# Five more items of the head each carry a step of a weight conversion, in a kernel of attention and two MLPs

## The chip, the cores and the metric

One core of a Trainium2 chip runs the whole program. The metric is the device time of one execution in microseconds; lower is better. The engines are PE (matrix products), DVE, ACT and POOL (elementwise work) and SP (which only issues transfers). Each engine has its own instruction stream and works it off in order. Sixteen DMA engines move the data.

## The reference

Causal attention with a decaying bias, then a leaky MLP, then four experts that are weighed by probabilities:

```python
scores = scale * np.matmul(q, k.transpose(0, 1, 3, 2))          # 2 batches, 8 heads, 576 positions, 64 wide
cum = np.cumsum(np.maximum(s, 0.0), axis=-1)
scores = np.where(causal, -1e9, scores + np.minimum(-(cum[..., :, None] - cum[..., None, :]), 0.0))
attn = softmax(scores)
x = matmul(attn, v)                                              # laid out as 1152 tokens x 512
h = x @ w_in                                                     # 512 x 2048
x = np.maximum(0.01 * h, h) @ w_out                              # 2048 x 512
for e in range(4):
    out += p[:, e:e + 1] * (np.maximum(x @ w1[e], 0.0) @ w2[e])
```

`w_in` and `w_out` come as 64-bit floats. The kernel gets their bits as pairs of 32-bit words and makes 32-bit floats of them on the chip: this is the conversion that the change is about.

## The kernel before, in words

**Attention as items.** Attention is cut into 16 units: a pair of heads of one batch, units 0 to 7 for positions up to 256, units 8 to 15 for the rest. A unit of the first kind has four items, one of the second kind five (its first item is the short last tile of both heads). `attention()` (line 1005) runs over the items `i` and issues, by the table `STEPS` (line 1003), different steps of different items together: the scores of item i on PE, followed by a mask and a row minimum on DVE (tile `z`), the exponentials of item i-1 on ACT (`z` in place), the transposes of item i-3 on PE (`ps_pt`) with their copies on ACT (`pv`), the products with the values of item i-5 (`ps_o`), and what ends a unit after that (`xo`, `ps_x`, `x`). It yields three times per item; between the yields its caller puts other work.

**The head.** The caller's first loop (line 1069 and on) runs over items 0 to 39 and is called the head here. Up to item 17 it puts idle products on PE, from item 24 on, by the table `OPENED`, the first steps of the MLP (`ps_u<-x,w`, three products of 512 columns each), from item 31 on two idle products more per item. At the third yield of an item it calls the conversion's generator once, if the item's number stands in the table `CONVERTING`, and at every item from 31 on.

**The woven stage.** The second loop runs over the items that are left, to 79. It puts about one step of the MLP's first half at two of the three yields, and calls the conversion at two yields of most items. When attention is over, the MLP goes on alone; its second half works on sums and differences of x (tile `t`) that DVE makes in `paired_steps`.

**The conversion.** `supply()` (line 151) converts 16 pieces of 128 x 1024 numbers, one step per call: the absolute value on ACT (`raw<-r`), two steps that clamp and shift on DVE (TENSOR_SCALAR on `raw`), two that join the low and the sign bits on DVE (SCALAR_TENSOR_TENSOR `raw<-r,raw`). The input `r` of a piece is fetched by `fetch64` (line 122) with two buffers: the fetch of piece n+2 is issued right behind the writing of piece n to memory (`w_f<-raw`, in `send`), on ACT's queue while `heading` is true, on POOL's queue after it. In the head the sending and splitting of piece n stand between the first and the second step of piece n+1, so that a piece takes seven calls there and six in the woven stage.

**The split.** A product needs a weight as a rounded part and a rest: a cast on ACT (`w<-raw`) and a subtraction on DVE (`w<-raw,w`). A piece that is next in line while one of the four weight buffers (`WB`) is free is split by `supply` straight from `raw`. Otherwise `late_splits()` (line 128) reads it back from memory on SP's queue (`raw<-w_f`) and splits it in two halves.

**The order.** All of this part is issued in the order in which the program is written (`InOrder`, line 28), so the tables decide what stands behind what on each engine. A profile names every such instruction by the one line 43.

Of the kernel before, what the change touches and what calls it, by code (L numbers as in the profile page):

```python
# [19 lines left out]
def attention_moe_moe2(ctx: ExitStack, tc: tile.TileContext, q, k, v, s, w_in, w_out, probs, w1, w2, out):  # L20
# [107 lines left out]
    def late_splits():  # L128

        nonlocal reading  # L130
        while len(ready) < CONVERTED:
            n = len(ready)
            if n < min(retired + WB + 2, stored):
                reading, raw = True, kept.pop(n, None)
                if raw is None:
                    raw = load_w(*stream[n][:3])
                    for _ in range(5):
                        yield
                while n >= retired + WB:
                    yield  # L140

                w = wpool.tile([P, 2, 1024], F32R, tag="w", name="w")
                for part in (slice(0, 512), slice(512, 1024)):
                    nc.scalar.copy(w[:, 0, part], raw[:, part])
                    (nc.gpsimd if n == CONVERTED - 1 else nc.vector).tensor_tensor(w[:, 1, part], raw[:, part], f32(w[:, 0, part]), ALU.subtract)
                ready.append(w.rearrange("p l (a b) -> p l a b", a=stream[n][1][0]))
                reading = False
            else:
                yield
# [900 lines left out]
    with ExitStack() as phase:  # L1050
# [3 lines left out]

        OPENED = (24, 25, 26, 27, 28, 29, 31, 33, 35)

        CONVERTING = (*range(5, 16), *range(17, 31, 2))
        side, units_of_w, late, opened = attention(), supply(), late_splits(), 0
        nothing = ps_mm.tile([P, 512], F32, tag="mm", name="nothing")
        with tc.tile_pool(name="early", bufs=1) as early:  # L1060
# [5 lines left out]
            for at_ in range(3 * 64):  # L1066
# [13 lines left out]
                if at_ % 3 == 2:  # L1080
                    if i == 3:
                        fetch64(1)
                    if i in (3, 4, 5):
                        next(sums)
                    if i in CONVERTING or i >= 31:
                        next(units_of_w)
# [109 lines left out]
```

## Time and profile before

| | |
|---|---|
| median of 3 runs | 698.78 us (698.61 to 701.58) |
| the profiled execution | 699.07 us, of which the span from the first to the last instruction is 697.3 us |
| PE busy | 677.7 us, 97% of the span |
| DVE, ACT, POOL busy | 475.8, 352.5, 406.0 us |
| mean granted clock of PE | 0.998 |

Times in the trace are counted from the start of the span. Busy time of PE is made of matmuls whose ends are modelled, so a busy PE may still hold short waits; a gap that the trace shows is real idle time. A row of a timeline gives start, length, engine, instruction, how many are merged in it, and in brackets the idle time before it and what ended that. A wait for several events is put down to the one that came last.

### The profile page before, as it was taken

The numbers are of one execution on the slowest core, as the hardware profiler recorded it, in microseconds if no ns is written. First come the engines' busy times: TensorE is split into PE (matmuls) and PEld (weight loads), VectorE is DVE, ScalarE is ACT, GpSimd is POOL, SyncE is SP. The second block draws the span as 40 slices with busy tenths as digits, with TensorE's granted clock in tenths as the row PEclk, the third lists the DMA queues.
The fourth block names the chain that finished last, engine by engine and source line by source line (L and its number), as shares of the span: only waits on it lengthen the run. The fifth ranks groups of instructions, "written<-read, shape, count | busy, mean of one in ns | idle before, by whom it ended". The sixth has DMA issues, their size and how long they took to land.

```text
span 697.3 us, 12008 instructions
## 1 busy us (share of the span) xinstructions
PE 677.7 (97%) x4496; PEld 623.7 (89%) x4496; DVE 475.8 (68%) x1040; ACT 352.5 (51%) x727; POOL 406.0 (58%) x386
## 2 busy tenths in 40 slices
PE   8899999899998999999999999999999999999998
PEld 7778778778787999999999989999899899998997
DVE  6878899998697458837855747647657376465564
ACT  5768978876544566533634525325244253261520
POOL 5100212221198887861997949949679498495830
PEclk9999999999999999999999999999999999999999
DMA  7798689746631321101011110111202111112003
GB/s 217 197 244 205 198 224 276 218 154 211 241 122 62 121 91 62 62 1 61 1 61 62 61 61 30 63 31 61 61 1 62 61 34 58 32 62 61 1 16 120
DMA packets 43050, 69.15 MB, mean 99 GB/s; under 512 B 6432, under 2 KB 26672, under 8 KB 42992
## 3 DMA queue, kind: packets, MB, share of 16 engines
q1 hardware_dynamic: 33744, 40.30, 19.9%
q0 software_dynamic: 6016, 20.71, 9.6%
q10 hardware_dynamic: 3232, 7.38, 3.3%
q8 instruction: 35, 0.57, 0.4%
q14 instruction: 23, 0.19, 0.1%
HBM read 57.54 MB, written 10.82 MB: 98 GB/s over the span
## 4 chain that ended last, share of the span: by engine, by line
PE 71%; DVE 8%; issue 8%; DMA 7%; ACT 3%; POOL 2%; SPq 0%; ACTq 0%; POOLq 0%; DVEq 0%
PE ps_d L43 35%; PE ps_u L43 33%; DMA r<-in_moe_w_out_dram 3%; DVE t L43 2%; DMA qr<-in_q_dram 2%; DMA r<-in_moe_w_in_dram 1%; PE ps_sc L43 1%; DVE sums L43 1%; DVE raw L43 1%; PE ps_o L43 1%; DVE z L43 1%; PE ps_pt L43 1%; DMA ke<-cum 1%; ACT raw L43 1%; DVE y L43 1%
## 5 line engine op out<-in xcount | busy, mean ns | idle before, releaser
L43 PE MATMUL ps_u<-t,w 128*128 128x320 f32 (+1 forms) x1680 | 237.7, 301 | 4.1 <-DVE t L43 2.9
L43 POOL TENSOR_TENSOR w<-raw,w 128x512 fp32r<-128x512 f32 (+2 forms) x118 | 185.9, 1595 | 94.2 <-ACT w L43 93.9
L43 PEld LDWEIGHTS ps_u<-t,w 128*128 128x128 f32 x1680 | 231.4, 191 | 5.5 <-DVE t L43 3.2
L43 PE MATMUL ps_d<-w,ht 128*128 128x256 f32 (+1 forms) x1164 | 195.4, 326 | 0.1
L43 PEld LDWEIGHTS ps_d<-w,ht 128*128 128x128 f32 x1164 | 173.3, 190 | 18.6 <-PE ps_u L43 0.4
L43 ACT CAST w<-raw 128x512 fp32r<-128x512 f32 (+2 forms) x138 | 98.2, 740 | 127.0 <-PE ps_d L43 69.7
L43 ACT ACTIVATE ht<-ps_u 128x320 fp32r<-128x320 f32 (+2 forms) x160 | 68.6, 439 | 99.2 <-DVE ps_u L43 71.1
L43 PE MATMUL ps_d<-ht,w 128*128 128x320 f32 (+1 forms) x576 | 109.1, 340 | 0.2 <-DVE ht L43 0.2
L43 PEld LDWEIGHTS ps_d<-ht,w 128*128 128x128 f32 x576 | 91.4, 188 | 6.6 <-DVE ht L43 0.6
L43 POOL TENSOR_TENSOR raw<-raw 128x256 f32<-128x256 f32 x120 | 86.2, 741 | 1.9
L43 DVE SCALAR_TENSOR_TENSOR oacc<-ps_d,pn,oacc 128x256 f32<-128x256 f32 (+1 forms) x92 | 51.5, 578 | 44.9 <-PE ps_d L43 44.2
L43 DVE TENSOR_TENSOR ps_u<-ps_u,tmp 128x320 f32<-128x320 f32 (+1 forms) x120 | 55.8, 469 | 31.5 <-PE ps_u L43 29.9
L43 DVE SCALAR_TENSOR_TENSOR ht<-ps_u,ht 128x320 fp32r<-128x320 f32 (+1 forms) x112 | 49.8, 455 | 16.8 <-ACT ht L43 16.5
L43 DVE TENSOR_TENSOR tmp<-ps_u,tmp 128x320 f32<-128x320 f32 (+1 forms) x80 | 36.9, 462 | 32.0 <-PE ps_u L43 24.5
L43 POOL DMA_DIRECT2D w_f<-raw x13 | 8.3, 637 | 85.3 <-DVE raw L43 71.8
L43 PE MATMUL ps_u<-x,w 128*128 128x512 f32 x192 | 55.7, 410 | 0.9 <-DVE x L43 0.9
L43 ACT ACTIVATE z<-z,mn 128x256 f32<-128x256 f32 (+4 forms) x72 | 42.5, 590 | 8.7 <-DVE mn L43 7.8
L43 DVE TENSOR_TENSOR ht<-ps_u,ht 128x320 fp32r<-128x320 f32 (+1 forms) x48 | 26.5, 553 | 26.8 <-ACT ps_u L43 26.6
L43 DVE CUSTOM_DVE_ANT_0 z<-ps_sc,mask 128x256 f32<-128x256 f32 (+4 forms) x72 | 35.9, 499 | 10.1 <-PE ps_sc L43 6.6
L43 POOL TENSOR_TENSOR ht<-sums,ht 128x1024 fp32r<-128x1024 f32 x16 | 38.6, 2409 | 6.3 <-ACT ht L43 6.3
L43 ACT COPY pv<-ps_pt 128x512 f32<-128x512 f32 (+3 forms) x80 | 33.2, 424 | 15.8 <-PE ps_pt L43 15.7
L43 PE MATMUL ps_pt<-ident,z 128*128 128x128 f32 x200 | 34.6, 276 | 5.9 <-ACT pv L43 4.9
(97 smaller groups left out, 773.5 us busy)
## 6 DMA issues: line engine op xcount, KB each, us to landing
raw<-in_moe_w_dram SPq DMA_DIRECT2D x32, 512.0 KB
raw<-w_f SPq DMA_DIRECT2D x21, 512.0 KB
w_f<-raw POOLq DMA_DIRECT2D x13, 512.0 KB, 3.5
r<-in_moe_w_out_dram POOLq DMA_DIRECT2D x6, 1024.0 KB, 8.6
r<-in_moe_w_in_dram POOLq DMA_DIRECT2D x5, 1024.0 KB, 8.4
r<-in_moe_w_in_dram ACTq DMA_DIRECT2D x3, 1024.0 KB
kd<-in_k_dram POOLq DMA_DIRECT2D x8, 288.0 KB, 7.6
kr<-in_k_dram SPq DMA_DIRECT2D x8, 288.0 KB
```

Source lines behind the costliest of these rows:

```text
L43: ins = call(*args, **kw)
```

## The change

Items 18, 20, 22, 24 and 26 of the head carry a call of the conversion too. Nothing else is edited.

```diff
-        CONVERTING = (*range(5, 16), *range(17, 31, 2))
+        CONVERTING = (*range(5, 16), *range(17, 28), 29)
```

The head then makes 31 calls in place of 26, and each later call comes five calls earlier against the items. Piece 2 (counted from 0) begins at item 18 instead of 19 and ends at item 24 instead of 31; piece 3 begins at item 25 instead of 32; the first three steps of piece 4 lie in the head. The order of PE's instructions is the same before and after. On SP the transfers `raw<-w_f` grow from 21 to 26, since pieces 4, 5, 8, 9 and 10 go through `late_splits` now; on ACT's queue `w_f<-raw` grows from 3 to 4 and `r<-in_moe_w` from 5 to 6, on POOL's queue they shrink by one each.

**First place: ACT at items 18 to 20.** `x0` is an output of attention, `raw_502` (`raw_487` in the change) is piece 2, `raw_347` piece 1, `r64` the 64-bit input. Before:

```order
L43 CAST x0_108<-ps_x_483 128x256
L43 ACTIVATE z_472<-z_472,mn_473 128x128
L43 COPY pv0_102<-ps_pt_497 128x256
L43 ACTIVATE raw_502<-r64_363 128x1024
L43 ACTIVATE z_487<-z_487,mn_488 128x128
L43 COPY pv0_102<-ps_pt_520 128x256
L43 ACTIVATE z_514<-z_514,mn_515 128x256
L43 COPY pv1_103<-ps_pt_536 128x128
L43 DMA w_f32_76<-raw_347 128x1024
L43 DMA r64_543<-in_moe_w_out_dram 128x2x1024
L43 CAST w_545<-raw_347 128x1024
```

In the change:

```order
L43 CAST x0_108<-ps_x_483 128x256
L43 ACTIVATE raw_487<-r64_363 128x1024
L43 ACTIVATE z_472<-z_472,mn_473 128x128
L43 COPY pv0_102<-ps_pt_499 128x256
L43 DMA w_f32_76<-raw_347 128x1024
L43 DMA r64_505<-in_moe_w_out_dram 128x2x1024
L43 CAST w_507<-raw_347 128x1024
L43 ACTIVATE z_489<-z_489,mn_490 128x128
L43 COPY pv0_102<-ps_pt_525 128x256
L43 ACTIVATE z_519<-z_519,mn_520 128x256
L43 COPY pv1_103<-ps_pt_542 128x128
```

The absolute value of piece 2 stands ahead of one exponential and one copy more, and the cast of piece 1 stands two exponentials and two copies earlier.

**Second place: DVE at items 21 to 24.** Before:

```order
L43 TENSOR_TENSOR xo_528<-ps_o_467,st_525 128x256
L43 ISA z_530,mn_531<-ps_sc_532,mask_93 128x256
L43 ISA mn_531 128x1
L43 ISA z_548,mn_549<-ps_sc_550,mask_93 128x128
L43 ISA mn_549 128x1
L43 ISA z_563,mn_564<-ps_sc_565,mask_93 128x128
L43 ISA mn_564 128x1
L43 TENSOR_TENSOR x0_108<-ps_x_559,x0_108 128x256
L43 TENSOR_TENSOR w_545<-raw_347,w_545 128x1024
```

In the change:

```order
L43 TENSOR_TENSOR xo_533<-ps_o_467,st_530 128x256
L43 TENSOR_TENSOR w_507<-raw_347,w_507 128x1024
L43 ISA z_536,mn_537<-ps_sc_538,mask_93 128x256
L43 ISA mn_537 128x1
L43 TENSOR_SCALAR raw_487<-raw_487 128x1024
L43 ISA z_550,mn_551<-ps_sc_552,mask_93 128x128
L43 ISA mn_551 128x1
L43 TENSOR_SCALAR raw_487<-raw_487 128x1024
L43 ISA z_566,mn_567<-ps_sc_568,mask_93 128x128
L43 ISA mn_567 128x1
L43 TENSOR_TENSOR x0_108<-ps_x_561,x0_108 128x256
L43 SCALAR_TENSOR_TENSOR raw_487<-r64_363,raw_487 128x1024
```

The subtraction of piece 1 stands ahead of item 21's `z` instead of behind item 23's, and steps of piece 2 stand between the `z` rows that followed each other before.

**Third place: ACT in the woven stage, unit 14.** `pv0` of 128x4x2x64 is the first copy out of the five transposes of a unit's first item. Before:

```order
L43 COPY pv1_103<-ps_pt_1877 128x384
L43 ACTIVATE z_1863,sums_1791<-z_1863,mn_1864 128x512
L43 ACTIVATE raw_1921<-r64_1824 128x1024
L43 COPY pv0_102<-ps_pt_1923 128x4x2x64
L43 COPY pv0_102<-ps_pt_1929 128x2x64
L43 ACTIVATE z_1907,sums_1791<-z_1907,mn_1908 128x384
L43 COPY pv0_102<-ps_pt_1947 128x4x128
```

In the change:

```order
L43 COPY pv1_103<-ps_pt_1900 128x384
L43 CAST w_1926<-raw_1846 128x512 x2
L43 ACTIVATE z_1886,sums_1815<-z_1886,mn_1887 128x512
L43 COPY pv0_102<-ps_pt_1948 128x4x2x64
L43 COPY pv0_102<-ps_pt_1954 128x2x64
L43 ACTIVATE z_1933,sums_1815<-z_1933,mn_1934 128x384
L43 COPY pv0_102<-ps_pt_1972 128x4x128
```

The absolute value `raw_1921` stood right ahead of this copy; in the change the cast of a piece that was read back, in two halves, stands there, behind no transfer of the 64-bit input. At unit 9 the absolute value of piece 4, which stood ahead of the same copy, stands in the head now and nothing takes its place; at unit 12 a cast in two halves stands ahead of the copy where only an exponential did.

## Rows read from the trace of the kernel before

**Rows 1.** The page: busy time by engine, and the last chain by line.

```profile
PE 677.7 (97%) x4496; PEld 623.7 (89%) x4496; DVE 475.8 (68%) x1040; ACT 352.5 (51%) x727; POOL 406.0 (58%) x386
...
PE ps_d L43 35%; PE ps_u L43 33%; DMA r<-in_moe_w_out_dram 3%; DVE t L43 2%; DMA qr<-in_q_dram 2%; DMA r<-in_moe_w_in_dram 1%; PE ps_sc L43 1%; DVE sums L43 1%; DVE raw L43 1%; PE ps_o L43 1%; DVE z L43 1%; PE ps_pt L43 1%; DMA ke<-cum 1%; ACT raw L43 1%; DVE y L43 1%
```

**Rows 2.** Windows: length, busy PE, PEld, DVE, ACT, POOL, clock, DMA share, GB/s.

```profile
32.97:48.45 15.48, 14.16 (x95) 12.38 (x95) 10.74 (x36) 11.47 (x32) 0.00 (x0) 1.00 1.01 252
...
60.00:190.00 130.00, 125.95 (x821) 101.93 (x820) 113.78 (x230) 99.76 (x205) 27.46 (x45) 1.00 0.72 211
...
190.00:217.00 27.00, 23.89 (x108) 19.65 (x107) 25.45 (x27) 13.61 (x22) 23.67 (x18) 1.00 0.34 122
```

**Rows 3.** Waits of PE up to 220 us: total, times, longest.

```profile
PE ps_pt L43 <- ACT pv L43: 4.9, 6, 1.7
...
PE ps_u L43 <- DVE t L43: 2.9, 1, 2.9
```

**Rows 4.** Timeline of ACT, items 10 to 20: start, length (us), idle before.

```profile
21.05 0.45 ACTq L43 DMA_DIRECT2D r<-in_moe_w_in_dram  x1
...
30.75 0.40 ACT L43 ACTIVATE z<-z,mn 128x128 f32<-128x128 f32 x1
...
31.06 0.36 ACT L43 COPY pv<-ps_pt 128x256 f32<-128x256 f32 x1
...
31.91 1.13 ACT L43 ACTIVATE raw<-r 128x1024 f32<-128x1024 f32 x1 [0.49 <-DMA r<-in_moe_w_in_dram]
...
34.05 1.05 ACT L43 CAST w<-raw 128x1024 fp32r<-128x1024 f32 x1
```

**Rows 5.** Timeline of DVE, items 21 to 30.

```profile
32.97 0.41 DVE L43 CUSTOM_DVE_ANT_0 z<-ps_sc,mask 128x256 f32<-128x256 f32 x1
...
36.30 1.21 DVE L43 TENSOR_TENSOR w<-raw,w 128x1024 fp32r<-128x1024 f32 x1
...
39.02 0.69 DVE L43 TENSOR_SCALAR raw<-raw 128x1024 f32<-128x1024 f32 x1
...
46.01 1.21 DVE L43 SCALAR_TENSOR_TENSOR raw<-r,raw 128x1024 uint32<-128x1024 uint32 x1
```

**Rows 6.** Windows of the instructions on raw: length, busy DVE, ACT, POOL.

```profile
32.97:48.45 15.48, 3.80 (x4) 1.12 (x2) 0.00 (x0) 1.00 1.01 252
```

**Rows 7.** Timeline of PE, gaps of the head from item 23.

```profile
35.71 0.44 PE L43 MATMUL ps_pt<-ident,z 128*128 128x128 f32 x2 [0.70 <-ACT pv L43]
...
48.93 0.50 PE L43 MATMUL ps_u<-x,w 128*128 128x512 f32 x1 [0.91 <-DVE x L43]
...
56.98 0.66 PE L43 MATMUL ps_pt<-ident,z 128*128 128x128 f32 x4 [0.58 <-ACT pv L43]
...
58.38 0.30 PE L43 MATMUL ps_pt<-ident,z 128*128 128x128 f32 x1 [0.75 <-DVE x L43]
```

**Rows 8.** Timeline of PE, gaps of the woven stage.

```profile
71.99 0.66 PE L43 MATMUL ps_pt<-ident,z 128*128 128x128 f32 x4 [0.40 <-ACT pv L43]
...
87.82 0.66 PE L43 MATMUL ps_pt<-ident,z 128*128 128x128 f32 x4 [0.56 <-ACT pv L43]
...
137.53 0.66 PE L43 MATMUL ps_pt<-ident,z 128*128 128x128 f32 x4 [1.70 <-ACT pv L43]
...
154.48 0.66 PE L43 MATMUL ps_pt<-ident,z 128*128 128x128 f32 x4 [1.00 <-ACT pv L43]
```

**Rows 9.** Timeline of ACT, two conversions of the woven stage.

```profile
152.77 1.19 ACT L43 ACTIVATE raw<-r 128x1024 f32<-128x1024 f32 x1 [2.25 <-DMA r<-in_moe_w_out_dram]
...
183.61 1.14 ACT L43 ACTIVATE raw<-r 128x1024 f32<-128x1024 f32 x1 [5.51 <-DMA r<-in_moe_w_out_dram]
```

**Rows 10.** Timelines of DVE and PE, end of the first MLP half.

```profile
202.78 0.69 DVE L43 TENSOR_TENSOR ht<-ps_u,ht 128x512 fp32r<-128x512 f32 x1 [0.97 <-ACT ps_u L43]
...
217.04 5.16 PE L43 MATMUL ps_u<-t,w 128*128 128x320 f32 x23 [2.92 <-DVE t L43]
```

**Rows 11.** Windows just behind that gap, columns as in Rows 2.

```profile
218.00:222.00 4.00, 4.00 (x19) 4.00 (x18) 1.49 (x4) 1.11 (x4) 3.98 (x4) 0.58 0.00 0
```

## The prediction

> **What bounds the kernel now.** I read the page first, then windows of all engines, then PE's waits and the timelines round its longest gaps. The page says that PE is busy for 677.7 of 697.3 us [rows 1]: 19.6 us of gaps are all that better order can win, anywhere. The windows show where they lie in the stretch that the change touches [rows 2]. Between item 21 and the end of the head's first half PE is busy for 14.16 of 15.48 us, in the woven stage for 125.95 of 130.00, in the 27 us round the end of the MLP's first half for 23.89. DVE is close behind: 113.78 of 130.00 in the woven stage. The list of PE's waits is the third view [rows 3]. Copies of transposes (`pv`, on ACT) cost it 4.9 us, DVE's `t` 2.9 us, and no converted weight stands in it. So PE does not wait for the conversion's results. The change can act only by what its steps stand ahead of on ACT and DVE, and by its transfers.
>
> The last chain names the transfers of the 64-bit weights with 3% and 1% of the span [rows 1], some 28 us. That chain runs through the conversion because its links follow each other closely, while PE beside it is nearly full; I return to it among the rivals.
>
> **The change, step by step.** No arithmetic is added; five calls move from the woven stage into items 18 to 26.
>
> *1. Item 18.* The input of piece 2 was asked for at 21.05 and ACT waited for it until 31.91, with 0.49 us of idling left [rows 4]. It took 10.9 us, and its issue is not moved, so it lands at 31.9 in the change too. Before, one exponential (0.40) and one copy (0.36) ran ahead of that wait; now they stand behind it. The subtraction of piece 1 now stands ahead of item 21's `z`, and it needs the cast, which stands behind all of them. That `z` can start at 31.91 + 1.13 + 0.40 + 0.36 + 1.05 + 1.21 = 36.06, in place of 32.97 [rows 4, 5]: 3.1 us late.
> The Trainium skill's page "DMA: Bandwidth & Descriptors" (section Bandwidth) has a measured 6.15 us for 1 MB. By that the input would be there before ACT asks, at 30.8, where the exponential ran instead; the chain would be 1.1 us shorter and the whole sum 1.1 us lower; the trace disagrees, with 10.9 us at a DMA share of about 1.0.
>
> *2. To the end of the first half.* PE's first MLP tile waits there for DVE's `x`, at 48.93 with a gap of 0.91 [rows 7]. From item 21's `z` to that `x` the conversion took 3.80 us of DVE in four instructions [rows 6]. In the change six stand there: three of 0.69 and three of 1.21 [rows 5], 5.7 us, so 1.9 more. DVE idled for 15.48 - 10.74 = 4.74 us in this stretch [rows 2]. If all of that can be used, `x` is late by 3.1 + 1.9 - 4.74 = 0.3 us; if none, by 5.0. I take 1.9, which uses 3.1 of the 4.74: most of that idling lay between items that PE paced, but the cast of piece 2 repeats the pattern of step 1 at item 27 and keeps DVE waiting once more. PE is nearly full here and cannot catch up by itself. **+1.9, from +0.3 to +5.0.**
>
> *3. Items 32 to 39.* Two gaps of PE, 0.58 for a copy and 0.75 for `x` [rows 7], lay where ACT was doing the absolute value of piece 3 and the cast of piece 2, 1.13 and 1.05 us with the lengths of their like [rows 4]. Both are gone from there, and the same two kinds of piece 4 come later, where only the idle products fill PE. **-0.4, from -1.3 to 0.**
>
> *4. The woven stage.* PE's four gaps, 0.40, 0.56, 1.70 and 1.00 us [rows 8], all stand behind a unit's five transposes, whose copies were late on ACT. What stood ahead of the copies at the first was the absolute value of piece 4, which is in the head now: -0.40. At the fourth it was an absolute value that had waited 2.25 us for its input [rows 9]; now it is a cast without such a wait: -1.0. At the other two a cast of 1.05 is exchanged for an absolute value of 1.13 or the reverse, 0. At unit 12 a cast is new: I put 0.2 on it, since ACT's copies there had slack. **-1.2, from -3.7 (all four gone) to +2.3 (one more wait of 2.25 ahead of a copy).** The five pieces that are read back add 5 transfers of 512 KB on SP and cost nothing in this sum: the DMA share is 0.72 [rows 2], and their splits end before PE needs them, since no weight is in its waits. If SP holds a load of attention behind one, that shows as a wait of ACT, for which the end of +2.3 stands.
>
> *5. The end of the conversion.* ACT waited 5.51 us for the last input [rows 9]. It will not, since that input is fetched five calls earlier, but PE had work of its own all through that time. Of the small gaps there I take **-0.2** (from -0.4 to 0).
>
> *6. The gap of 2.92 us at 217* [rows 10]. It ends DVE's chain of sums and rests for the second half of the MLP. That chain starts behind PE's own products: `ht` at 202.78 had waited for ACT, which had waited for PE. In the 27 us round it DVE is busy for 25.45 [rows 2]. An earlier conversion doesn't move its start against PE, and the order behind it is the same. **0, from -2.9 to 0.**
>
> Sum: +1.9 - 0.4 - 1.2 - 0.2 = +0.1. The profiled execution took 699.07 us, so this gives 699.2; the median of the runs, 698.78, lies 0.3 below it, so I forecast **698.9**. All ends together would be 690.8 and 706.1; they will not come together. The forecast's own range is 696.5 to 701.5.
>
> **Rivals.** *A. The conversion is the bound after all* (faster). For it speaks the last chain, with 28 us of weight transfers. Then the gaps of the woven stage go (4.05 us between 60 and 190) and the one of 2.92 with its clock, and the head hides its steps. 698.8 - 4.1 - 2.9 + 0.3 = **692.1**, or about 695 without the second gap. Against it: no wait of PE names a weight, and the chain of step 6 starts on PE. Chance 0.08.
>
> *B. DVE's order in the head costs its full price* (slower). Place: item 21's `z` and every item up to the `x` at 48.45. The 4.74 us of DVE's idling cannot be used, since it is spent waiting for ACT's cast, and nothing comes back later: 698.8 + 5.0 = **703.8**. It decides against me once that `x` runs more than 3.5 us later than it did. For it: two ends of a chain through ACT and DVE stand ahead of a `z` that ran free. Against it: PE had been waiting in just this place already, 0.70 us at 35.71. Chance 0.12.
>
> *C. PE's clock falls in the head.* After the 2.92 us gap the granted clock was 0.58 between 218 and 222 [rows 11], a mixture of the lower level of 1.2 GHz and the full 2.4; that lost 4 x 0.42 = 1.7 us. From item 18 to 24 the head has neither idle products nor MLP steps, so the 3.1 us of step 1 make PE thinner just there, in several short gaps. If it falls once, the time is 698.9 + 1.7 = **700.6**. The Trainium skill (page "TensorE: Matmul & The Clock Gate", Part 1) says that the slow clock is the default and activity releases it; the trace agrees, with 0.58 behind the longest gap. Against it: behind the gap of 1.70 in the woven stage the clock did not leave 1.00 (60 to 190 [rows 2]). Chance 0.10.
>
> *D. The moved steps meet nothing.* Head and woven stage are both paced by PE, and delays die out in the items' lags: **698.8**, with 0.5 either way. Chance 0.10. The forecast has 0.60.
>
> **How the numbers follow.** A measurement of this kernel can tell about 0.5% from no change, 3.5 us: faster means under 695.3, slower over 702.3. A gives faster 0.08. B gives slower 0.12. C, D and the forecast lie within, 0.80. The range goes from 696.0 to 702.3: it takes in C, D and the forecast's own range and leaves out A and most of B.
>
> **What would show it.** Right: in the head, item 21's `z` about 3 us later, behind the subtraction; the `x` near 48.45 about 2 us later; the first gap of the woven stage gone and the last one smaller; no wait of about 5 us of ACT near 183; a gap of nearly 3 us still ahead of the first `ps_u<-t`. Wrong: that gap shrunk to under 1 us, the clock below 1.00 between 30 and 50, a wait of PE for `w`, or an `x` that is late by over 3.5 us.

## The result, and the profile after

The change takes 705.9 us (median of 6 runs, 703.3 to 707.3) where the kernel before takes 698.76 (6 runs, 698.6 to 701.6): 1.0098 times as long, with an interval of 1.0073 to 1.0123. That is 7.1 us more, twice what a measurement can tell, and above the range that was predicted (696.0 to 702.3). The profiled execution took 705.83 us, with a span of 704.1 against 697.3.

The page has nearly the same totals as before [rows 1]: no work was added, so the 6.8 us are time in which work stood or ran slowly. PE is busy 3.6 us longer for the same 4496 products, and idle 3.2 us longer (22.8 in place of 19.6).

```profile
PE 681.3 (97%) x4496; PEld 625.9 (89%) x4496; DVE 473.0 (67%) x1045; ACT 353.2 (50%) x732; POOL 404.8 (57%) x384
```

The same windows as in [rows 2], by time from the span's start:

```profile
32.97:48.45 15.48, 11.73 (x70) 9.17 (x70) 8.95 (x25) 7.95 (x22) 0.00 (x0) 1.00 1.04 259
60.00:190.00 130.00, 122.70 (x801) 99.58 (x800) 113.63 (x235) 101.18 (x215) 26.41 (x43) 0.99 0.75 226
```

From 33 to 48.5 us PE, DVE and ACT all do less than before in the same time (PE 11.73 in place of 14.16). When every engine is less busy, none of them is the one that is too slow; it points to something outside them that holds them up. The DMA share is 1.04 (1.01 before).

PE's timeline in the head shows where, the rows that answer to [rows 7]:

```profile
42.51 0.44 PE L43 MATMUL ps_pt<-ident,z 128*128 128x128 f32 x2 [1.39 <-ACT pv L43]
47.92 0.33 PE L43 MATMUL ps_pt<-ident,z 128*128 128x128 f32 x1 [2.06 <-ACT pv L43]
49.76 0.81 PE L43 MATMUL ps_o<-vs,pv 128*128 128x65 f32 x4 [0.80 <-issue]
63.87 0.45 PE L43 MATMUL ps_pt<-ident,z 128*128 128x128 f32 x1 [1.99 <-DVE x L43]
```

Up to 40 us the change runs nearly as before: item 21's `z` starts at 33.86, against 32.97. The first two gaps are ACT's. Its timeline from item 18 on:

```profile
30.04 1.15 ACT L43 ACTIVATE raw<-r 128x1024 f32<-128x1024 f32 x1
...
30.68 0.68 ACTq L43 DMA_DIRECT2D r<-in_moe_w_out_dram  x1
...
40.79 1.12 ACT L43 ACTIVATE raw<-r 128x1024 f32<-128x1024 f32 x1 [2.31 <-DMA r<-in_moe_w_out_dram]
41.82 0.49 ACT L43 ACTIVATE z<-z,mn 128x256 f32<-128x256 f32 x1
42.22 0.24 ACT L43 COPY pv<-ps_pt 128x128 f32<-128x128 f32 x1
...
45.39 0.35 ACTq L43 DMA_DIRECT2D w_f<-raw  x1
...
46.27 1.04 ACT L43 CAST w<-raw 128x1024 fp32r<-128x1024 f32 x1 [3.54 <-DMA qr<-in_q_dram]
47.22 0.40 ACT L43 ACTIVATE z<-z,mn 128x128 f32<-128x128 f32 x1
```

Read it from the brackets. Piece 3's input is asked for at 30.68, behind piece 1's store. At item 25 ACT wants it, stands 2.31 us, and gets it at 40.79, after 10.1 us; the exponential (41.82) and the copy (42.22) that PE waits for stand behind it. Then ACT is idle for 3.54 us more: the store of piece 2 goes out only at 45.39, the next fetch behind it, and the cast starts at 46.27. An exponential and the copies come after that, and PE's gap of 2.06.

The releaser of the second wait is a load of queries, with which the store has nothing to do. The program's order explains it: transfers of SP and ACT take eight semaphores in turn, and an issue waits for the transfer that had its semaphore before. Three of them stand on the same one:

```
ACT  DMA r64_505<-in_moe_w_out_dram 128x2x1024 [waits DMAHW5_49]
SP   DMA qr_579<-in_q_dram 64x2x256 [waits DMAHW5_49]
ACT  DMA w_f32_76<-raw_487 128x1024 [waits DMAHW5_49]
```

So SP's load waits for piece 3's input (its list of waits has 3.6 us, once, for that transfer), and the store waits for SP's load. The times agree: the load goes out at 40.78, when ACT has its input (40.79). SP's timeline shows its side, four loads in one row, which began at 38.26 before:

```profile
36.77 0.37 SPq L43 DMA_DIRECT2D vs<-in_v_dram  x1
40.78 2.55 SPq L43 DMA_DIRECT2D qr<-in_q_dram  x4
```

(The Trainium skill, page "DMA: Bandwidth & Descriptors", section "Why a DMA increments its semaphore by 16 and not by 1", asks for a semaphore of its own for each transfer in flight, since two on one can be mistaken for each other. The waits above keep to that with eight of them, and 3.54 us is the price that the trace shows for it here; what the page warns of, a wait that ends too early, no run here shows.)

DVE stands with ACT, for the cast, and is late at `x`:

```profile
47.34 1.22 DVE L43 TENSOR_TENSOR w<-raw,w 128x1024 fp32r<-128x1024 f32 x1 [4.16 <-ACT w L43]
...
53.17 0.42 DVE L43 TENSOR_TENSOR x<-ps_x,x 128x256 fp32r<-128x256 f32 x1
```

That is the `x` which stood at 48.45 before: 4.7 us late. Then the clock. Windows behind the gaps, with the granted clock in the third column from the right:

```profile
50.00:54.00 4.00, 4.00 (x22) 3.92 (x22) 3.31 (x9) 2.37 (x8) 0.00 (x0) 0.57 0.88 290
54.00:58.00 4.00, 4.00 (x29) 3.78 (x28) 3.03 (x10) 2.45 (x7) 0.00 (x0) 1.00 0.33 94
64.00:68.00 4.00, 4.00 (x20) 3.71 (x20) 1.07 (x3) 2.06 (x5) 0.58 (x1) 0.61 0.74 223
```

It fell behind the gaps at 47 to 50 us and behind the one of 1.99, and lost 4 x 0.43 = 1.7 and 4 x 0.39 = 1.6 us. Before, it was 1.00 all the way from 33 to 217 us.

The woven stage and its end, the rows that answer to [rows 8] and [rows 10]:

```profile
94.92 0.66 PE L43 MATMUL ps_pt<-ident,z 128*128 128x128 f32 x4 [0.72 <-ACT pv L43]
110.72 0.33 PE L43 MATMUL ps_pt<-ident,z 128*128 128x128 f32 x1 [1.65 <-ACT pv L43]
128.23 0.66 PE L43 MATMUL ps_pt<-ident,z 128*128 128x128 f32 x4 [0.38 <-ACT pv L43]
145.89 0.66 PE L43 MATMUL ps_pt<-ident,z 128*128 128x128 f32 x4 [1.52 <-ACT pv L43]
...
223.75 6.49 PE L43 MATMUL ps_u<-t,w 128*128 128x320 f32 x32 [1.88 <-DVE t L43]
```

The gap of 1.65 is new. ACT's timeline ahead of it has a cast that waited for a piece which was read back:

```profile
104.99 1.14 ACT L43 CAST w<-raw 128x512 fp32r<-128x512 f32 x2 [2.47 <-DMA raw<-w_f]
```

The account of the two profiles: gaps of the head that answer to each other, 0.70 + 0.91 + 0.58 + 0.75 = 2.94 before and 0.26 + 1.39 + 2.06 + 0.80 + 1.99 = 6.50 after, +3.6 (0.26 at 35.09). The copies' gaps in the woven stage, 3.66 before and 4.27 after, +0.6. The gap ahead of `t`, -1.0. Two more falls of the clock, +3.3. Together +6.5 of the 6.8.

The runs agree with it. Each lists its span and its mean granted clock c, and span x (1 - c) is about the time that the clock lost (704.1 x 0.007 = 4.9 in the profiled run; three falls of some 1.7 in its trace). Means over the runs of a kernel:

| kernel | median us | ratio to before, interval | lost to the clock | span without that |
|---|---|---|---|---|
| before (28 runs beside e9 to e12) | 698.25 | | 1.7 | 694.8 |
| the change | 705.9 | 1.0098, 1.0073 to 1.0123 | 5.5 | 698.5 |
| e1 two of the five calls | 700.79 | 1.0039, 1.0016 to 1.0063 | 3.3 | 696.2 |
| e2 calls of 25 and 26 later | 705.35 | 1.0080, 1.0058 to 1.0102 | 5.7 | 696.9 |
| e3 change, POOL's queue | 705.48 | 1.0108, 1.0092 to 1.0125 | 4.6 | 699.6 |
| e4 before, POOL's queue | 697.71 | 0.9987, 0.9970 to 1.0003 | 1.3 | 694.6 |
| e5 e2 and e3 together | 704.33 | 1.0080, 1.0051 to 1.0108 | 4.6 | 697.1 |
| e6 two DVE steps earlier | 703.85 | 1.0081, 1.0049 to 1.0112 | 4.9 | 697.0 |
| e7 cast further behind its load | 705.19 | 1.0088, 1.0058 to 1.0117 | 5.1 | 697.1 |
| e8 combined | 704.04 | 1.0082, 1.0049 to 1.0114 | 5.1 | 696.5 |
| e9 before, work alone | 699.6 | 1.0016, 0.9994 to 1.0038 | 1.75 | 695.8 |
| e10 before, bytes alone | 702.59 | 1.0063, 1.0038 to 1.0088 | 5.0 | 695.6 |
| e11 before, three calls fewer | 701.04 | 1.0037, 1.0015 to 1.0059 | 3.5 | 695.9 |
| e12 change, idle products | 704.9 | 1.0124, 1.0081 to 1.0168 | 5.4 | 699.0 |
| e13 change, two inputs left out | 701.72 | 1.0039, 1.0013 to 1.0065 | 3.7 | 696.6 |
| e14 before, two inputs left out | 697.28 | 0.9985, 0.9965 to 1.0005 | 1.6 | 694.0 |
| e15 e6 and e12 together | 707.02 | 1.0120, 1.0092 to 1.0149 | 4.7 | 700.4 |
| e16 e13 and POOL's queue | 699.39 | 1.0010, 0.9986 to 1.0034 | 2.5 | 695.3 |
| e17 e16 and e6 together | 701.58 | 1.0047, 1.0014 to 1.0080 | 4.6 | 696.0 |
| e18 e4 again | 697.53 | 0.9980, 0.9955 to 1.0005 | 1.5 | 694.2 |

Half of what the change costs (5.5 - 1.7 = 3.8) is the clock, the other half (698.5 - 694.8 = 3.7) in the main PE standing. Each ratio is to runs of the kernel before that were measured beside its own (one set each for e1 to e4, e5 to e8, e9 to e12, e13 to e15, e16 to e18). One slow run each of e7 and e8 is left out of the ratio and of the last two columns.

### The profile page after: what moved, and what is told of

It is laid out like the page before. It is cut to its first block, busy times and chain, and to the rows that moved or that the text cites. A ratio compares the mean times of both kernels' runs of the same rounds, so it can differ in the third digit from the quotient of the medians.

```text
span 704.1 us, 12028 instructions
## 1 busy us (share of the span) xinstructions
PE 681.3 (97%) x4496; PEld 625.9 (89%) x4496; DVE 473.0 (67%) x1045; ACT 353.2 (50%) x732; POOL 404.8 (57%) x384
## 4 chain that ended last, share of the span: by engine, by line
PE 72%; DVE 11%; DMA 7%; issue 5%; ACT 3%; POOL 1%; SPq 0%; ACTq 0%; POOLq 0%; DVEq 0%
PE ps_d L43 35%; PE ps_u L43 34%; DMA r<-in_moe_w_out_dram 2%; DVE raw L43 2%; DVE t L43 2%; DVE z L43 1%; DVE sums L43 1%; PE ps_o L43 1%; DMA r<-in_moe_w_in_dram 1%; DMA kr<-in_k_dram 1%; DMA raw<-w_f 1%; DMA w_f<-raw 1%; ACT w L43 1%; PE ps_sc L43 1%; PE ps_pt L43 1%
## 5 line engine op out<-in xcount | busy, mean ns | idle before, releaser
L43 PEld LDWEIGHTS ps_pt<-ident,z 128*128 128x128 f32 x200 | 24.9, 142 | 20.4 <-ACT pv L43 12.4
```

The costliest lines, as they stand in the source:

```text
L43: ins = call(*args, **kw)
```

## The experiments

**e1. Two of the five calls.**

```diff
-        CONVERTING = (*range(5, 16), *range(17, 28), 29)
+        CONVERTING = (*range(5, 16), *range(17, 22), 23, 25, 27, 29)
```

> Edit: of the five added calls only those at items 18 and 20; piece 2 still begins one item early, but piece 3's absolute value, which the change has at item 25, comes at item 29, and piece 2's send after item 31. Theory T (a chain of DMA waits): in the change ACT stands 2.31 us at item 25 for piece 3's input, SP stands 3.6 us behind the same transfer because its next load shares a semaphore with it, that load lands late, and ACT then stands 3.54 us with piece 2's send, which shares a semaphore with that load. Here the input has landed (40.7 in the change) long before the absolute value (about 45 us), so both waits of ACT go, only SP's stays, off the path: 698.0 to 700.5 us, clock 1.00 from 50 to 54. Rival R (more work of the conversion on DVE between items' steps costs, whatever the transfers do): two of five calls, 700.5 to 703.

700.79 us, just inside what rival R expects. ACT's absolute value of piece 3 came at 44.94 without a wait, but ACT stood 3.00 us at the store of piece 2 all the same, now for a load of `kd`, and the clock fell at 52 us (0.57 from 52 to 56), behind a gap of PE of 1.50. One of the two waits went, the other only moved.

**e2. The same number of calls, those of items 25 and 26 at 28 and 30**, and **e3. The change with POOL's queue.**

```diff
-        CONVERTING = (*range(5, 16), *range(17, 28), 29)
+        CONVERTING = (*range(5, 16), *range(17, 25), *range(27, 31))
```

> Edit: all 31 calls in the same items but for three: the calls at 25, 26 and 29's predecessor are moved so that items 25 and 26 have none and 28 and 30 have one; piece 3's absolute value comes at item 27 in place of 25. The amount of work that the conversion has in the head is that of the change. Theory T: the input of piece 3 has landed before item 27 (about 42.5 us), ACT's wait of 2.31 goes, and the send comes some 3 us later too, so that little of its 3.54 is left: 699.5 to 702 us, gaps of PE at 42.5 and 47.9 gone or under 0.7 each. Rival R (work on DVE): the same 31 calls, closer together behind item 27: 705 to 708. Rival K (the clock alone): as T, but only if the clock stays at 1.00 from 50 to 54; if gaps go and the clock falls all the same, 703 to 704.

```diff
-            queue = nc.scalar if heading else nc.gpsimd
+            queue = nc.scalar if heading and n == 0 else nc.gpsimd
```

> Edit: the change, but from piece 1 on the conversion's sends and the fetches behind them go through GpSimd's queue in the head, as they do later, instead of ACT's; calls and items are those of the change. Theory T: the transfers have no semaphore in common with SP's loads any more, so SP does not stand 3.6 us for piece 3's input and ACT does not stand 3.54 us with the send; the 2.31 us at item 25 stays, since the input is asked for at the same time: 700.5 to 703 us, PE's gap at 42.5 stays, those at 47.9 and 49.8 go. Rival B (bandwidth: the head's transfers are simply too many for the stretch from 30 to 52 us): the loads land as late as they do in the change and 704.5 to 707 results. Rival R (work on DVE): 705 to 707.

705.35 and 705.48: theory T missed both times, and the rivals of work and (in e3) of bandwidth had these times. In e3 the shared semaphore was gone, as meant, and SP no longer stood for the input. But ACT had that input 3 us later. Two of the three come from the queue: POOL issues the fetch behind two loads of `kd` and the store, 2.1 us later than ACT did. The third is a longer transfer, 11.1 us in place of 10.1, beside SP's loads. The timelines of POOL and ACT, and PE's gap behind them:

```profile
32.74 0.71 POOL L43 DMA_DIRECT2D r<-in_moe_w_out_dram  x1
```

```profile
43.83 1.12 ACT L43 ACTIVATE raw<-r 128x1024 f32<-128x1024 f32 x1 [4.40 <-DMA r<-in_moe_w_out_dram]
```

```profile
45.55 0.44 PE L43 MATMUL ps_pt<-ident,z 128*128 128x128 f32 x2 [3.48 <-ACT pv L43]
```

One wait of 4.40 took the place of 2.31 and 3.54. In e2 the wait for the input was down to 0.66 and the one at the store to 1.13, but SP still stood 4.2 for the input; PE stood 1.96 us for ACT's copies and 2.39 for `kd`, and the clock was at 0.50 from 54 to 62 us. So neither edit freed PE: one made the other wait longer, the other left SP's loads late.

**e4. The control of the queue.** The edit of e3 on the kernel before.

> Edit: the kernel before with the same edit of the queue as the run on the change with GpSimd's queue; a control for what the queue does by itself. Theory T: before the change ACT's two waits do not exist, SP's two waits on the conversion's input (3.0 us in total) go, which are off the path: 698.0 to 699.3 us. Were GpSimd's queue itself better or worse for the transfers, the time would move by over 1 us here too, and the third run would have to be read against that.

697.71, no difference that can be told: the queue costs nothing in a kernel in which ACT does not stand for that input. In e3, where it does, the later fetch counts.

**e5. Both edits at once** (e2's table, e3's queue).

> Edit: both earlier edits of the change at once: piece 3's absolute value at item 27 in place of 25 (31 calls in the head as in the change), and the head's sends and fetches from piece 1 on through GpSimd's queue. It is the fourth corner of a square whose other three (the change 705.9, calls later 705.35, queue 705.48) are all slow. Theory T2 (ACT, which works in order, must not stand for a transfer, and there are two such waits: for piece 3's input, removed by the first edit, and for a semaphore shared with SP's loads, removed by the second; either one alone is enough to cost the time): both gone, PE has no gap over 1 us between 40 and 58, the head gives back 3 to 4 us: 701 to 703. Rival R (31 calls of work on ACT and DVE are too many in this head wherever they stand): 705 to 707. Rival B (transfers saturate the DMA engines from 30 to 52 us and PE starves of keys and queries): 705 to 707 with PE's or SP's waits on qr, kr or kd instead.

704.33, at best 1.5 us better. The input came at 43.50, after ACT had stood 1.86 us for it at item 27, and the gap of 2.00 for DVE's `x` near 61 us and its fall of the clock stayed. So this was no case without waits; the expectation had counted on an input at 40.8.

**e6. DVE's two steps of items 32 and 33 at 28 and 30.**

```diff
-        CONVERTING = (*range(5, 16), *range(17, 28), 29)
+        CONVERTING = (*range(5, 16), *range(17, 31))
...
-                    if i in CONVERTING or i >= 31:
+                    if i in CONVERTING or i >= 31 and i not in (32, 33):
```

> Edit: the change, but the two calls at items 32 and 33 (the two three-operand steps of piece 3 on DVE) move to items 28 and 30, so that piece 3 ends at item 31 and DVE has no conversion work at 32 and 33; all else in its item, transfers too. Theory T2's second part: in the change PE waits 1.99 us at 63.87 for DVE's x, which those two steps delay, and its clock falls behind it (0.83 between 60 and 70, 1.7 us): the gap shrinks to under 1, the clock stays at 1.00 from 60 to 70, 702 to 704. Rival: the gap follows from the lateness of the items before it (waits at 42 to 50), and DVE catches up at 28 to 31 no better: 705 to 707, gap as before.

703.85, as expected, but its ratio's interval overlaps the change's. PE's timeline shows that the gap near 62 shrank as expected, and that it opened again at another `x`, where the steps stand now:

```profile
55.26 0.50 PE L43 MATMUL ps_u<-x,w 128*128 128x512 f32 x1 [1.81 <-DVE x L43]
63.61 0.30 PE L43 MATMUL ps_pt<-ident,z 128*128 128x128 f32 x1 [0.43 <-DVE x L43]
```

**e7. Seven steps between a load and its cast in the woven stage**, and **e8. The edits of e3 and e7, with 28 calls** (none at items 25 to 27, 32 and 33, one each at 28 and 30).

```diff
-                    for _ in range(5):
+                    for _ in range(7):
```

> Edit: the change, but in the woven stage the cast of a piece that is read back stands seven of the stage's steps behind its load in place of five. Theory T2's third part: in the change ACT stands 2.47 us at 105 for a piece that is read back (there are five more of these than before), which makes PE's gap of 1.65 at 110.7: that gap goes and 704.0 to 705.0 results. Rival: the reads cost nothing of their own, as I predicted, and PE's gap moves elsewhere: 705.5 to 706.5.

> Edit: GpSimd's queue for the head's sends and fetches from piece 1 on, piece 3's absolute value at item 28, no call at items 32 and 33 (28 calls in the head: two more than before the change), and seven steps in place of five between a load and its cast. Theory T2: all three costs gone, so at or under the kernel before: 695 to 698.5. Rival R: two calls more than before, in a denser part: 699 to 702.

705.19 and 704.04, both misses; e8 lies above both of its expectations. In e7's profile the gap at 110 is gone, but one of 3.13 us stands at 149; in e8's there is one of 4.13 at 129. Ahead of these stands no read-back but an absolute value that waited for its 64-bit input, 1.84 us in e7 and 5.73 in e8. ACT's timeline of e8:

```profile
127.61 1.12 ACT L43 ACTIVATE raw<-r 128x1024 f32<-128x1024 f32 x1 [5.73 <-DMA r<-in_moe_w_in_dram]
```

The edits that aimed at one gap left another in its place.

**e9. Work alone, and e10. Bytes alone,** both on the kernel before.

```diff
+            junk = early.tile([P, 384], F32, name="junk")
+            tc.nc.gpsimd.memset(junk, 0.0)
...
+                    if i in (18, 22, 26):
+                        for _ in range(2):
+                            nc.vector.tensor_tensor(junk, junk, junk, ALU.subtract)
+                    if i in (20, 24):
+                        for _ in range(2):
+                            nc.scalar.copy(junk, junk)
```

> Edit: the kernel before, with five pieces of plain work in the head and no transfer: at items 18, 22 and 26 two subtractions of 128x384 on DVE (about 1.1 us together), at items 20 and 24 two copies of 128x384 on ACT (about 0.95), on a tile of its own that nothing reads; they stand where the change's five calls stand. Rival R (each call costs because its work stands ahead of an item's step in the order of DVE or ACT; two calls cost 2.4 us, five cost 7.1): about 1 us for each piece, 701.5 to 704. Theory T (the wait for transfers costs, not the work): 697.5 to 699.5.

```diff
+    spare = dram.tile([3, P, 1024], F32, name="spare")
...
+                    if i in (20, 23, 26):
+                        nc.gpsimd.dma_start(spare[(i - 20) // 3], w2[0][(i - 20) // 3 * 2 * P : ((i - 20) // 3 * 2 + 2) * P, :].rearrange("(k p) f -> p k f", p=P))
```

> Edit: the kernel before, with three transfers of 1 MB in the head from DRAM to DRAM (read and written, so at least the bytes that the change moves forward into 30 to 52 us) through GpSimd's queue at items 20, 23 and 26, which nothing waits for; no work on DVE or ACT. Rival B (the DMA engines are full there, so that more bytes make SP's loads of queries and keys, and with them PE, late): 701 to 706, with the falls of the clock that follow such gaps. Rival R (work): 697.5 to 699.

This pair decided the direction. Work where the calls stand: 699.6, +1.1, not clear of noise, and no more loss to the clock than before (1.75 against 1.7). Transfers that nothing waits for: 702.59, +4.4, of which 3.3 are the clock. ACT's timeline shows the way it goes, and PE's and the windows what follows:

```profile
47.52 0.72 ACT L43 CAST qs<-qr 128x640 fp32r<-128x640 f32 x1 [5.07 <-DMA qr<-in_q_dram]
```

```profile
48.57 0.48 PE L43 MATMUL ps_pt<-ident,z 128*128 128x128 f32 x1 [2.56 <-ACT pv L43]
```

```profile
50.00:54.00 4.00, 4.00 (x17) 3.62 (x16) 3.81 (x9) 2.63 (x8) 0.00 (x0) 0.50 1.14 239
```

The loads of queries are issued when they were before, but their cast on ACT starts at 47.52 in place of 43.06; PE stands behind ACT, and the clock falls. The bytes here are more than the change's, and POOL issued all three transfers between 32 and 34 us, so 4.4 is not the change's share. But that transfers alone reach PE by way of ACT is shown without any call of the conversion.

**e11. The opposite of the change**, three calls fewer than before.

```diff
-        CONVERTING = (*range(5, 16), *range(17, 31, 2))
+        CONVERTING = (*range(5, 16), *range(17, 25, 2))
```

> Edit: the kernel before, but without the calls at items 25, 27 and 29: the opposite of the change, 23 calls in the head in place of 26. Rival R (a call in the head costs over 1 us, in the woven stage less): 694 to 696.5. My prediction's view (the conversion comes in time, the head is filled without loss): 698 to 699.5. Were the conversion the bound at its end, PE's gap ahead of the first use of t (2.92 us before, 1.88 with the change) would grow to over 4 us: 699.5 to 701.

701.04, slower too. The gap ahead of `t` did not grow (2.92), so the conversion's end is no bound, and the calls that moved into the woven stage made a gap there, where 0.56 stood before [rows 8]. Ahead of it ACT's absolute value waited for its input, as in the head of the change:

```profile
87.18 1.13 ACT L43 ACTIVATE raw<-r 128x1024 f32<-128x1024 f32 x1 [1.78 <-DMA r<-in_moe_w_in_dram]
```

```profile
88.83 0.65 PE L43 MATMUL ps_pt<-ident,z 128*128 128x128 f32 x4 [2.26 <-ACT pv L43]
```

23, 26, 28 and 31 calls in the head give 1.0037, 1, 1.0039 and 1.0098: the time has its least near the kernel before.

**e12. Idle products on PE in items 25 to 28**, and **e15. The same with e6's edit.**

```diff
+                if at_ % 3 == 0 and 25 <= i < 29 and opened:
+                    for _ in range(3):
+                        nc.tensor.matmul(held[0][:, :P], idle[:, :P], idle[:, :P], start=False, stop=False, skip_group_check=True)
```

> Edit: the change, with three idle products (0.2 us each, on zeros) ahead of the transposes of each of the items 25 to 28, where PE waits 1.39 and 2.06 us in the change; their twelve cost 2.3 us at most, and nothing where they lie in those gaps. Theory K (half of the loss is the clock: its records show 0.50 for 3.4 us behind each of the gaps at 47.9 and 62, 1.7 us each): the fall at 50 us goes and the runs' mean clock rises from about 0.992 to 0.994 or more: 703.5 to 705. Rival: the fall comes with or without them: 706 to 708.

> Edit: the change with both edits that aimed at a gap with a fall of the clock behind it: no calls at items 32 and 33 (they stand at 28 and 30), and three idle products ahead of the transposes of the items 25 to 28. Theory K (these two gaps make the falls): the mean clock rises from 0.992 to 0.996 or more, 701 to 703. Rival: the falls come behind other gaps of this head just as well, since it has more of them: clock 0.992 to 0.994, 703.5 to 706.

704.9 and 707.02; e12's median lies in the range of theory K, its ratio (1.0124) above the change's. In the two profiled executions it looks as hoped: e12's gaps near 43 and 48 us are 0.62 and 0.40 and the clock is 1.00 up to 60 us, in e15 it is 1.00 from 16 to 220. Over the runs it is not so: the clock's loss was 5.4 and 4.7 us against 5.5, and the span without it grew to 699.0 and 700.4. Theory K, that these two gaps make the falls, is not borne out; and one profile would have misled here.

**e13. The change without the inputs of pieces 3 and 4** (their buffers are set to zero, so two pieces' values are left out), **and e14. The same of the kernel before.**

```diff
+        if n in (3, 4):
+            nc.gpsimd.memset(r64, 0)
+            return
```

> Edit: the change, but the inputs of pieces 3 and 4 are not loaded; their buffers are set to zero by GpSimd instead (this leaves 2 MB of loads in the head out, and the converted values of two pieces). Calls, their work and the stores are those of the change. Theory T (the calls are dear since they need transfers early, in a stretch in which the DMA engines are full: ACT stands for them, SP's loads come late, the clock falls behind the gaps): 697.5 to 700.5, clock 0.996 or higher, no gap of PE above 1 us from 40 to 52 us. Rival R (the calls' real work and its chains between ACT and DVE): 703.5 to 706, gaps at 42 to 50 as in the change.

> Edit: the kernel before with the same two loads left out: the control. Both theories: 696 to 698.5, since before the change ACT did not stand for these loads; what it gains here is what the loads' bytes cost even there. T and R are told apart by the distance between this run and the one on the change: under 2.5 us by T, over 5 by R.

701.72 and 697.28. The distance of the ratios is 0.0054 (3.8 us), against 0.0098 (6.8) with the inputs: between the expectations. In e13 one of the two waits was left, with the store of piece 2, as ACT's timeline shows, and PE's gap behind it:

```profile
43.73 0.35 ACTq L43 DMA_DIRECT2D w_f<-raw  x1
44.12 1.04 ACT L43 CAST w<-raw 128x1024 fp32r<-128x1024 f32 x1 [2.64 <-DMA qr<-in_q_dram]
```

```profile
45.78 0.33 PE L43 MATMUL ps_pt<-ident,z 128*128 128x128 f32 x1 [1.35 <-ACT pv L43]
```

**e16. e13 with the queue of e3.** Here the input does not load and the store shares no semaphore: both waits are gone at last.

> Edit: the change without the loads of pieces 3 and 4 (buffers set to zero, two pieces' values left out), and the head's stores and fetches from piece 1 on through GpSimd's queue. No instruction of ACT in items 18 to 31 waits for a transfer of the conversion, nor for a semaphore of one. Theory T (the two waits of ACT are the head's loss between 40 and 52 us): no gap of PE over 1 us from 38 to 56; 698.5 to 700.5; what is then left over the control (697.3) is the DVE gap near 62 and the woven stage. Rival R (work): 701 to 703, as the run without the inputs.

699.39, as theory T has it: all 31 calls with their casts, subtractions and joins stand in the head, and the kernel takes 1.0010 times the time before. ACT's cast of piece 2 runs without a wait. PE's gaps behind it, and ACT ahead of the last of them:

```profile
41.21 1.05 ACT L43 CAST w<-raw 128x1024 fp32r<-128x1024 f32 x1
```

```profile
48.04 0.50 PE L43 MATMUL ps_u<-x,w 128*128 128x512 f32 x1 [0.37 <-DVE x L43]
...
58.03 0.30 PE L43 MATMUL ps_pt<-ident,z 128*128 128x128 f32 x1 [1.99 <-DVE x L43]
...
105.92 0.33 PE L43 MATMUL ps_pt<-ident,z 128*128 128x128 f32 x1 [2.42 <-ACT pv L43]
```

```profile
100.24 1.14 ACT L43 CAST w<-raw 128x512 fp32r<-128x512 f32 x2 [3.59 <-DMA raw<-w_f]
```

From 36 to 56 us none is over 0.37. What is left over e14, 0.0025 or 1.7 us, would fit the other two, DVE's `x` and the read-back; the clock fell behind both (0.58 from 58 to 62, 0.57 from 106 to 110). But e14 is no control for the queue, which e4 put at 0.9987 by itself.

**e17. e16 with e6's edit, and e18. e4 again.**

> Edit: as the run before this one, and the calls of items 32 and 33 stand at 28 and 30. If the three places are what the change costs in the head, and add: 697 to 699, PE's gap near 62 under 1 us. If the woven stage pays besides (the five pieces more that are read back): 699.5 to 701.5 with a clean head.

> Edit: the kernel before with the head's stores and fetches from piece 1 on through GpSimd's queue, a repeat of the control. It was 0.9987 of the kernel before (0.9970 to 1.0003). If the queue is a gain of its own, 0.997 to 0.999 again; if not, 0.999 to 1.001.

e17 (701.58) is no faster than e16, though their intervals overlap: its gap near 61 is down to 0.42, but one of 1.80 stands at 49.73, as in e6, and the clock fell behind it. DVE's joins delay an `x` in either place. e18 came out at 0.9980 after 0.9987 in e4; both intervals still reach past 1, so a gain of some 1 us is likely and not shown. No run was clearly under the kernel before.

## Why the prediction was wrong

*What bounds the kernel.* Right as far as it went: PE is nearly full, no weight is waited for, and the change acts by what its steps stand ahead of and by its transfers. The transfers were then priced for one piece only.

*Step 1, item 18.* Mechanism there, size wrong. The subtraction does stand ahead of item 21's `z`, but the input of piece 2 had landed when ACT asked for it at 30.04, and the `z` came at 33.86, not 36.06.

*Step 2, to the end of the first half: the step that failed.* It says that "the cast of piece 2 repeats the pattern of step 1 at item 27 and keeps DVE waiting once more", and takes 1.9 for all. The cast was kept not by exponentials but by two transfers: DVE stood 4.16 us for it, and `x` was 4.7 us late. In place of 1.9, PE's gaps up to there grew by 2.9 us (1.61 to 4.51), and the fall of the clock behind them cost 1.7 more. Step 1 took 10.9 us for an input from [rows 4]. The same figure, from the issue of piece 3's input behind piece 1's store at about 31, gives 42, and ACT was to ask for it at 38.5: a wait of 3 us was there to be worked out, at item 25, and has no term in the sum. It was looked for where a wait had stood before, not where the calls make a new one. The store's wait for a shared semaphore could be seen in the program's order alone; the sum has no term for it either.

*Step 3, items 32 to 39.* Wrong sign. The copy's gap (0.58) went, as said, but the gap for `x` (0.75) became 1.99, since two joins of piece 3 now stand ahead of that `x`, and the clock fell behind it.

*Step 4, the woven stage.* The two gaps that were to go went (0.40 and 1.00). "Cost nothing" was wrong for the pieces that are read back: one kept ACT 2.47 us ahead of the gap of 1.65, which went when e7 gave the read-backs more time. The copies' gaps came to +0.6 in place of -1.2, inside the bounds.

*Steps 5 and 6.* ACT's wait of 5 us near 183 is gone and gave nothing, as said. The gap ahead of `t` shrank by 1.0, which was put at 0.

*The rivals.* A and D are out. B named the place and the test (`x` more than 3.5 us late: it was 4.7, against the 5.0 of its price), and had it that DVE's idling "is spent waiting for ACT's cast", which it was. Its cause was not DVE's order, though: e9 puts plain work there for 1.1 us and e16 the real one for 1.7, with intervals of about 2 us. C was right that the clock falls, though not where it looked, between items 18 and 24: the clock was 1.00 up to 50 us. It fell twice more in the change, not once, and the clock is half of the loss; the two were taken for alternatives and came together, both behind the same gaps.

*What the runs show of the cause.* In ratios to before: the change 1.0098, without the two inputs 1.0039 (control 0.9985), without the shared semaphore too 1.0010. So of 6.8 us about 3.0 go with the two inputs, 2.0 with the store's wait behind them, and 1.7 remain for DVE's `x` and the woven stage; each has its share of the clock in it. Only the first step, and the first two together, are clear of noise. The queue may have part of the second: it gave 0.9987 and 0.9980 by itself, some 1 us, and then the store's wait has nearer 1 and the rest nearer 3. That the steps don't add is shown by e3, where the second edit alone gave nothing (and brought the input later).

*Open.* Why the clock falls behind some gaps and not others; which of DVE's joins and the read-backs has how much of the last 1.7 us; and whether the two inputs cost by ACT's wait or by their bytes beside SP's loads, since e13 takes both away. An input of piece 3 that is fetched early enough was not tried; it would need a third buffer for `r`.

## What to carry to other kernels

A step that is moved forward takes its transfer's deadline with it. For each, write down when its input is asked for, add the longest duration that the trace shows for such a transfer in that stretch, and compare with the new time at which an in-order engine will want it; do it for every piece, not only for the one where a wait stands today. Then read in the program's order which semaphore each transfer issue waits for: an issue on a compute engine's queue can stop that engine for a load of somebody else. And allow for the clock behind a gap of PE, as a chance and not as a rule: here the clock was half of the loss, though gaps of over 3 us stand in e3 and e7 with no fall behind them.

## What was not expected of the hardware

The three slow stretches in the change's profile are alike, 1.6 to 1.7 us lost each. Others are longer: in e10 the windows from 46 to 58 us lose 3.4 together, and the granted clock is 0.50, the lower level of 1.2 GHz, where a window lies wholly in one. Behind the gap of 1.99 or 2.00 us near 60 us (the change, e3, e5, e7, e12, e13, e16) a fall followed in all seven profiles. Behind gaps of 1.70 to 1.76 us at 136 to 139 us (before, e4, e9, e14, e18) none followed, behind one of 2.45 in e15 none either, and behind the longest gaps of e3 and e7 none: after 3.48 the clock was 1.00 from 44 to 56 us, after 3.13 from 146 to 158. So the length of a gap does not settle it.

1 MB of input took 10.1 us in the change (30.68 to 40.79) and 11.1 in e3 (32.74 to 43.83), where SP's loads ran beside it; in the change the shared semaphore had kept part of them back. (The 6.15 us of the Trainium skill, page "DMA: Bandwidth & Descriptors", section Bandwidth, were met by neither, with the DMA share at about 1.0.) Transfers that nothing waits for cost 4.4 us (e10), work on DVE and ACT in the places of the calls 1.1, which is not clear of noise (e9).
